# Pooled attention and routed experts: VectorE's value sums as one strided reduction instead of a chain of additions

## Chip, cores and metric

The kernel runs on one core of a Trainium2 chip. The metric is the device time of one execution in microseconds; the time before is 616.48 us, the median of three runs (615.58 to 618.09). "PE" is TensorE's matmul, "PEld" its weight load, "DVE" VectorE, "ACT" ScalarE, "POOL" GpSimd and "SP" SyncE, as in the rows below.

## What is computed

Eight batches of attention (8 heads, 576 queries, head size 64) over keys and values that are first averaged in groups of 8, so that 72 are left, and then a layer of eight experts of which each token takes one:

```python
k_p = k.reshape(B, H, Sp, 8, D).mean(axis=3)
v_p = v.reshape(B, H, Sp, 8, D).mean(axis=3)
attn = softmax(q @ k_p.T / sqrt(D));  x = attn @ v_p      # 4608 tokens x 512
e_idx = argmax(x @ w_gate)
out = gate_w * sigmoid(x @ w_output_gate)[e_idx] * (relu(x @ w1[e_idx]) @ w2[e_idx])
```

The change touches only how the eight values of a group are summed (the division by 8 is done elsewhere).

## The kernel before

**Attention.** The 4608 queries are 36 tiles of 128. Each tile is worked in two halves (four heads each), so there are 72 half steps, and the code writes them out in the order in which every engine runs its part. In a half step PE computes the scores of tile i (line 266, into one of three banks p_h), transposes the probabilities of tile i-2 (line 286) and computes the value product of tile i-3 (line 294, into bank p_y[0] or p_y[1] by the half). VectorE takes the maximum of the scores (`peak`, line 272), and for tile i-3 the reciprocal of the row sums (`values`, line 310) and the product with it (`normalise`, line 316, output xg). ScalarE computes the exponentials and copies the transposed probabilities. A bank p_y is free for the value product two half steps later once line 316 has read it.

**Values.** The values of one batch lie in the buffer `vt` (a view of the tensor that the rows call `rows`): for each half `a` (0 or 1) and each of three groups `c` of partitions, 512 words, which are 8 neighbouring values of 64 words. Their sum is `vp` (3 x 64 words for each half). There is one buffer `vt`: SyncE's load of the next batch (`load_v`, line 191, six DMAs) waits until the last sum has read it, and behind it in SyncE's queue stand the loads of queries (line 187) and keys (line 183).

For batches 1 to 7 the first of three halvings is done by GpSimd (`halve_v`, line 225: three additions 128x256 for each half a). The other two are VectorE's (`pool_v`, line 229): four partial sums become two (`n = 2 * D`), and two become one (`n = D`, into `vp`). For batch 0 VectorE does all three (`first_v`), in the kernel's start.

**Order.** The generator `pooled` gives VectorE's additions of one batch one by one to a queue of spare work; `work(n)` takes n pieces from it, and a half step calls it with 2 pieces behind the maximum, 1 behind the value product and 1 behind the normalisation (`WORK = (2, 1, 1)`). `pooled(b)` is put at the head of the queue. Behind it stand the pieces of `route`, which choose the expert of a group of four tiles. The sum `vp` is then read by PE (`turn_v`, line 244) and ScalarE (`place_v`, line 239).

**After attention.** GpSimd has written the normalised rows into the experts' order (line 434), the last group's routing makes a table of jobs, and the expert stage (from 187 us on) runs over that table with PE's two layers (lines 1015 and 996).

Of the kernel before, what the change touches and what calls it, by code (L numbers as in the profile page):

```python
# [15 lines left out]
ALU = mybir.AluOpType  # L16
AX = mybir.AxisListType
PSUM = bass.MemoryType.PSUM

B, H, S, D = 8, 8, 576, 64  # L20
KEYS, POOL = 72, 8
# [75 lines left out]
def attention_and_routing(ctx, tc, sh, qT, kT, v, wg, wst, xs):  # L97
    nc = tc.nc
# [11 lines left out]
    vt = sh.rows[:, 0:6 * DM].rearrange("p (a c f) -> p a c f", a=2, c=3)  # L110
# [68 lines left out]
    k_t, vp_t, vT_t = {}, {}, {}  # L179
# [45 lines left out]
            nc.gpsimd.tensor_tensor(vt[:, a, c, 0:256], vt[:, a, c, 0:256], vt[:, a, c, 256:512], op=ALU.add)  # L225

    def pool_v(b, a, n):
        to = vt[:, a, :, 0:n] if n > D else vp_t[b][:, :, a]
        nc.vector.tensor_tensor(to, vt[:, a, :, 0:n], vt[:, a, :, n:2 * n], op=ALU.add)

    def first_v(a):
        if a == 0:
            vp_t[0] = p2.tile([P, 3, 2, D], F32, tag="vp", name="vp0", bufs=1)
        for n in (4 * D, 2 * D, D):
            pool_v(0, a, n)

    def place_v(b, c):
        for h in range(2):
# [282 lines left out]

    def pooled(b):
        for a in range(2):
            for n in (2 * D, D):
                pool_v(b, a, n)
                yield 0

    tick = [0]

# [14 lines left out]
    for b in range(1, B):  # L544
        f = S * b // P + 0.5 * (b % 2)
        at(f - 8.5, load_k, b)
        at(max(f - 5, 0), load_v, b)
        at(f - 4.5, load_q, b)
        for m in range(9):
            at(max(f - 5.5, 0) + 0.5 * (m // 2), add_k, b, *((4 >> m // 4, m % 4, m % 4 + 1) if m < 8 else (1, 0, 4)))  # L550
        at(max(f - 2.5, 1.5), scale_k, b)
        for a in range(2):
            at(f - 2.5 + 0.5 * a, halve_v, b, a)
        at(f - 2, lambda b: queue.insert(0, [pooled(b), 0, -1]), b)
        for c in range(3):
            at(f - 0.5 + 0.5 * c, place_v, b, c)
        at(f - 0.5, turn_v, b)
        at(f + 1.5, gate_v, b)
# [24 lines left out]
    prepare_counts()  # L583
    ready_k(0)
    first_v(0)
    at(-0.5, ready_k, 1)
    at(-0.5, first_v, 1)
    at(1.5, prepare_routing)
    for c in range(3):
# [822 lines left out]
```

## Time and profile before

| what | value |
|---|---|
| median of three runs | 616.48 us (615.58 to 618.09) |
| the profiled execution's own time | 617.31 us |
| its span, first to last instruction | 615.6 us |
| busy: PE, VectorE, ScalarE, GpSimd | 581.6, 361.5, 260.0, 234.6 us |
| attention with its start | to about 165 us |
| expert stage | from about 187 us |

The span leaves out 1.7 us around the first and the last instruction. A busy share is an average over stages with different limits, so the rows further down are taken from single stretches. Times in rows are in microseconds from the span's start, unless they are said to be ns. A bracket at a row's end is the time for which the engine sat idle before it, and what ended it. [...]

### The profile page before, as it was taken

How to read it: one execution, taken by the hardware profiler on the slowest of the kernel's cores; microseconds unless marked ns; L12 is line 12 of the kernel's file. 1: busy time of each engine (PE TensorE's matmuls, PEld its weight loads, DVE VectorE, ACT ScalarE, POOL GpSimd, SP SyncE). 2: the span in 40 equal slices, each digit the busy share in tenths (PEclk: the TensorE clock that was granted, in tenths of full speed). 3: DMA queues.
4: the chain of work that ended last, by engine and by line, in shares of the span. 5: the costliest groups of instructions: out<-in, count | busy, mean ns of one | idle time of the engine just before them, and what ended most of it. 6: DMA issues, size and time to landing. Idle time of an engine off the chain costs nothing.

```text
span 615.6 us, 12478 instructions
## 1 busy us (share of the span) xinstructions
PE 581.6 (94%) x3543; PEld 531.6 (86%) x3544; DVE 361.5 (59%) x836; ACT 260.0 (42%) x693; POOL 234.6 (38%) x348
## 2 busy tenths in 40 slices
PE   0899999998898999999989999999999999999996
PEld 0899998887897989899879988989898898989895
DVE  5678899877986823699377513376143843333232
ACT  2798887788542511367235201244031520211110
POOL 3667889782444533134131222212121331212031
PEclk9999999999999999999989999999999999999999
DMA  9878789899576641748848413073223203020112
GB/s 260 281 233 281 255 282 345 314 323 284 170 249 194 199 145 37 219 137 292 254 156 255 139 44 70 17 230 129 80 41 117 70 5 83 17 68 17 52 35 68
DMA packets 52622, 99.20 MB, mean 161 GB/s; under 512 B 7406, under 2 KB 31982, under 8 KB 50736
## 3 DMA queue, kind: packets, MB, share of 16 engines
q1 hardware_dynamic: 44560, 76.62, 41.5%
q0 software_dynamic: 7968, 21.63, 9.6%
q14 instruction: 72, 0.59, 0.3%
q8 instruction: 22, 0.36, 0.3%
HBM read 74.03 MB, written 25.51 MB: 162 GB/s over the span
## 4 chain that ended last, share of the span: by engine, by line
PE 64%; issue 3%; DVEq 1%; DVE 1%; POOL 0%; ACT 0%; POOLq 0%
PE p_h L1015 33%; PE p_y L996 30%; PE p_y L649 1%; DVEq L1189 0%; DVE rows L1186 0%; POOL out L1329 0%; DVE xt L1159 0%; DVEq L754 0%; DVE p_y L83 0%; DVEq L1158 0%; ACT xt L1086 0%; DVEq L774 0%; DVE ht L1195 0%; PE p_y L1052 0%; DVE sums L1213 0%
## 5 line engine op out<-in xcount | busy, mean ns | idle before, releaser
L1102 ACT ACTIVATE ht<-p_h 128x384 fp32r<-128x384 f32 (+1 forms) x104 | 46.8, 450 | 237.0 <-PE p_h L1015 226.4
L1329 POOL DMA_INDIRECT out<-rows,dst x41 | 42.2, 1030 | 209.5 <-DVE rows L1186 207.2
L1015 PE MATMUL p_h<-xt,w1b 128*128 128x384 f32 (+1 forms) x736 | 117.2, 320 | 3.3 <-DVE ht L1195 2.7
L1015 PEld LDWEIGHTS p_h<-xt,w1b 128*128 128x128 f32 x736 | 116.0, 192 | 4.5 <-DVE ht L1195 2.9
L996 PE MATMUL p_y<-w2b,ht 128*128 128x512 f32 x480 | 110.4, 390 | 0.0
L996 PEld LDWEIGHTS p_y<-w2b,ht 128*128 128x128 f32 x480 | 89.8, 188 | 18.4
L1195 DVE SCALAR_TENSOR_TENSOR ht<-p_h,ht 128x384 fp32r<-128x384 f32 (+1 forms) x104 | 52.3, 503 | 89.0 <-ACT ht L1102 82.2
L996 PE MATMUL p_y<-w2a,ht 128*128 128x512 f32 x408 | 94.5, 390 | 0.7 <-PE p_y L649 0.4
L1015 PE MATMUL p_h<-xt,w1a 128*128 128x256 f32 (+1 forms) x640 | 93.6, 306 | 0.6 <-DVE sums L1213 0.6
L1015 PEld LDWEIGHTS p_h<-xt,w1a 128*128 128x128 f32 x640 | 92.9, 190 | 1.4 <-DVE sums L1213 0.8
L1186 DVE TENSOR_SCALAR rows<-p_y,sc 128x512 f32<-128x512 f32 x41 | 30.6, 750 | 104.6 <-PE p_y L996 87.5
L996 PEld LDWEIGHTS p_y<-w2a,ht 128*128 128x128 f32 x408 | 76.1, 188 | 17.1 <-issue 1.6
L277 ACT ACTIVATE p<-p_h,m 128x72 f32<-128x72 f32 x288 | 71.4, 367 | 21.2 <-DVE m L272 20.8
L294 PE MATMUL p_y<-vbd,pT 128*128 128x162 f32 (+1 forms) x480 | 73.5, 306 | 6.1 <-DVE xg L316 4.4
L294 PEld LDWEIGHTS p_y<-vbd,pT 128*128 128x128 f32 (+1 forms) x480 | 60.7, 179 | 9.8 <-issue 5.9
L1306 POOL DMA_INDIRECT xm<-xs,src x54 | 55.8, 1034 | 26.4 <-POOL src L1302 13.4
L434 POOL DMA_INDIRECT xs<-xg,where x36 | 37.0, 1029 | 30.1 <-PE p_y L294 8.5
L210 POOL TENSOR_TENSOR kq<-kq 128x288 f32<-128x288 f32 (+1 forms) x63 | 41.3, 682 | 15.5 <-DMA kq<-kT 14.1
L266 PE MATMUL p_h<-kbd,q_even 128*128 128x144 f32 (+1 forms) x160 | 29.7, 314 | 14.5 <-DMA q_even<-qT 11.7
L287 ACT ACTIVATE pT<-ptr 128x384 f32<-128x384 f32 x72 | 38.0, 530 | 2.6 <-PE ptr L286 1.6
L266 PEld LDWEIGHTS p_h<-kbd,q_even 128*128 128x128 f32 (+1 forms) x160 | 23.8, 199 | 15.9 <-issue 12.1
L286 PE MATMUL ptr<-ident,p 128*128 128x128 f32 x216 | 36.4, 278 | 0.1
(174 smaller groups left out, 667.4 us busy)
## 6 DMA issues: line engine op xcount, KB each, us to landing
stage<-wst SPq DMA_DIRECT2D x64, 512.0 KB
kq<-kT SPq DMA_DIRECT2D x7, 1152.0 KB
rows<-xs SPq DMA_DIRECT2D x40, 192.0 KB
rows<-v SPq DMA_DIRECT2D x16, 288.0 KB
kq<-qT SPq DMA_DIRECT2D x4, 1152.0 KB
rows<-xs SPq DMA_DIRECT2D x64, 64.0 KB
q_even<-qT SPq DMA_DIRECT2D x3, 1152.0 KB
xs<-stage SPq DMA_DIRECT2D x8, 321.0 KB
```

The source lines that it names most:

```text
L210: nc.gpsimd.tensor_tensor(k[:, :, 0:w], k[:, :, 0:w], k[:, :, w:2 * w], op=ALU.add)
L266: nc.tensor.matmul(s[r0:r0 + n, 144 * c:144 * c + 144], q_t[b][:, 2 * a + c, s0:s0 + n], kbd[b % 2][:, 2 * a + c, :], start=True, stop=True)
L277: nc.scalar.activation(pt[i % 3][:, 4 * a + h, 0:KEYS], sv[:, h], AF.Exp, bias=m[:, h:h + 1])
L287: nc.scalar.activation(pT_t[i][:, 3 * a:3 * a + 3, :], tr[:, 0:384].rearrange("p (c n) -> p c n", c=3), AF.Copy)
L294: nc.tensor.matmul(av[r0:r0 + n, COLS * c:COLS * c + 2 * COLS], pT[:, 3 * a + c, r0:r0 + n], vbd[b % 2][:, a, c].rearrange("p h f -> p (h ...
L434: ins = nc.gpsimd.indirect_dma_start(out=xs, out_offset=bass.IndirectOffsetOnAxis(ap=where, axis=0), in_=x.bitcast(I32), in_offset=None)
L996: i = mm(to, ht[:, h, f, P * k:P * k + P], w[:, part, o:o + DM], start=(f == 0 and part == 0 and h == 0), stop=(f == 7 and h == 1))
L1015: i = mm(to, w[:, part, o:o + P], x, start=(d == 0 and k == 0), stop=(d == 3 and k == len(terms) - 1))
L1102: act(ht[:, 0, f, 0:n], p_h[f % 3][:, 0:n], AF.Relu).then_inc(q["hh"], 1)
L1195: nc.vector.scalar_tensor_tensor(ht[:, 1, f, 0:n], src, 0.0, ht[:, 0, f, 0:n].bitcast(F32), op0=ALU.max, op1=ALU.subtract).then_inc(q["hl" ...
L1306: nc.gpsimd.indirect_dma_start(out=xb[:, k].bitcast(I32), out_offset=None, in_=pairs_of, in_offset=bass.IndirectOffsetOnAxis(ap=src[:, k:k ...
L1329: nc.gpsimd.indirect_dma_start(out=out, out_offset=bass.IndirectOffsetOnAxis(ap=dst[:, k:k + 1], axis=0), in_=yb[2 if k == size - 1 else k ...
```

## The change

`pool_v` sums all partial sums of a half in one instruction, a `tensor_reduce` over a view in which the partial sums are the innermost axis (step 64 words) and the 64 words of a value the next one. Batch 0 sums 8 values per result in one instruction for each half where three additions stood; batches 1 to 7 sum 4 where two additions stood. GpSimd's halving stays as it is. `pooled` gives two pieces of work instead of four.

```diff
     def pool_v(b, a, n):
-        to = vt[:, a, :, 0:n] if n > D else vp_t[b][:, :, a]
-        nc.vector.tensor_tensor(to, vt[:, a, :, 0:n], vt[:, a, :, n:2 * n], op=ALU.add)
+        nc.vector.tensor_reduce(vp_t[b][:, :, a], vt[:, a, :, 0:n].rearrange("p c (r d) -> p c d r", d=D), axis=AX.X, op=ALU.add)

     def first_v(a):
...
-        for n in (4 * D, 2 * D, D):
-            pool_v(0, a, n)
+        pool_v(0, a, POOL * D)
...
     def pooled(b):
         for a in range(2):
-            for n in (2 * D, D):
-                pool_v(b, a, n)
-                yield 0
+            pool_v(b, a, POOL // 2 * D)
+            yield 0
```

On VectorE in the kernel's start, around the two sums of batch 0 (kq are keys, m the maxima of scores, the numbers after a name tell tiles apart), the order of before and then of after:

```order
L229 TENSOR_TENSOR rows<-rows 128x3x256
L229 TENSOR_TENSOR rows<-rows 128x3x128
L229 TENSOR_TENSOR vp_151<-rows 128x3x64
L272 TENSOR_REDUCE m_0_157<-p_h 128x4
L206 TENSOR_TENSOR kq<-kq 128x2x288
L206 TENSOR_TENSOR kq<-kq 128x2x144
L206 TENSOR_TENSOR kq<-kq 128x2x72
L229 TENSOR_TENSOR rows<-rows 128x3x256
L229 TENSOR_TENSOR rows<-rows 128x3x128
L229 TENSOR_TENSOR vp_151<-rows 128x3x64
L272 TENSOR_REDUCE m_1_174<-p_h 128x4
```

Here only the additions go and nothing else changes its place; the same stretch of VectorE after:

```order
L228 TENSOR_REDUCE vp_151<-rows 128x3x64
L270 TENSOR_REDUCE m_0_155<-p_h 128x4
L206 TENSOR_TENSOR kq<-kq 128x2x288
L206 TENSOR_TENSOR kq<-kq 128x2x144
L206 TENSOR_TENSOR kq<-kq 128x2x72
L228 TENSOR_REDUCE vp_151<-rows 128x3x64
L270 TENSOR_REDUCE m_1_170<-p_h 128x4
```

Each maximum m still follows directly on a sum. On VectorE in batch 6's sums, as in every batch from 1 to 7 (grec is the reciprocal, xg the normalisation), before:

```order
L229 TENSOR_TENSOR rows<-rows 128x3x128
L229 TENSOR_TENSOR vp_1623<-rows 128x3x64
L310 RECIPROCAL grec_1482<-p_y 128x4
L229 TENSOR_TENSOR rows<-rows 128x3x128
L316 TENSOR_TENSOR xg_1480<-p_y,grec_1482 128x320
L229 TENSOR_TENSOR vp_1623<-rows 128x3x64
L272 TENSOR_REDUCE m_1_1685<-p_h 128x4
```

The reciprocal and the normalisation stood between the additions of the first half and the last addition of the second; VectorE at the same place after:

```order
L228 TENSOR_REDUCE vp_1609<-rows 128x3x64 x2
L308 RECIPROCAL grec_1468<-p_y 128x4
L314 TENSOR_TENSOR xg_1466<-p_y,grec_1468 128x320
L270 TENSOR_REDUCE m_1_1669<-p_h 128x4
```

Now both halves' sums stand ahead of them, next to each other. Two line numbers less are the lines that the change takes out.

## Rows read from the trace of the kernel before

**Rows 1.** The page: the span, and the clock granted to TensorE in 40 slices of it (tenths of full speed, 9 is 90% or more).

```profile
span 615.6 us, 12478 instructions
PEclk9999999999999999999989999999999999999999
```

**Rows 2.** Busy time of each engine (with the number of instructions) in three stretches, in us from the span's start: attention, the passage to the experts, the experts. The last columns are the granted clock, the share of the DMA engines' time and GB/s.

```profile
18.00:140.00 122.00, 116.58 (x944) 108.59 (x942) 103.74 (x335) 100.38 (x381) 97.47 (x139) 1.00 0.87 290
140.00:187.00 47.00, 42.41 (x291) 39.27 (x291) 37.96 (x152) 28.82 (x86) 17.98 (x19) 1.00 0.67 219
187.00:615.60 428.60, 419.09 (x2299) 380.57 (x2299) 208.90 (x322) 126.72 (x216) 113.81 (x162) 1.00 0.38 114
```

**Rows 3.** Who waited for whom between 12 and 187 us: us in total, times, the longest in us.

```profile
DVE rows L229 <- POOL rows L225: 5.1, 6, 2.5
PE p_y L294 <- DVE xg L316: 4.4, 5, 1.5
```

**Rows 4.** The same view for the DMA queue of SyncE, up to 190 us.

```profile
SPq L191 <- DVE vp L229: 80.3, 7, 13.7
```

**Rows 5.** Groups of VectorE instructions up to 200 us with their shapes apart: output and input size, count, busy us, mean ns of one, idle us before them. The 128x768 additions are batch 0's first ones.

```profile
L332 DVE TENSOR_REDUCE lg<-xg 128x64 f32<-128x512 f32 x9 | 6.1, 676 | 0.0
...
L229 DVE TENSOR_TENSOR rows<-rows 128x768 f32<-128x768 f32 x2 | 1.9, 954 | 4.3 <-DMA rows<-v 4.3
L671 DVE TENSOR_REDUCE rows<-rows 128x100 f32<-128x700 f32 x1 | 1.5, 1509 | 0.0
L671 DVE TENSOR_REDUCE rows<-rows 128x12 f32<-128x84 f32 x1 | 0.3, 313 | 0.0
```

**Rows 6.** The timeline of all engines in the start: start us, duration us, engine, line, operation, count of merged instructions.

```profile
11.01 1.55 DVE L229 TENSOR_TENSOR rows<-rows 128x768 f32<-128x768 f32 x2 [4.28 <-DMA rows<-v]
...
12.60 0.36 DVE L229 TENSOR_TENSOR vp<-rows 128x192 f32<-128x192 f32 x1
...
13.46 1.58 DVE L206 TENSOR_TENSOR kq<-kq 128x576 f32<-128x576 f32 x3
...
14.96 1.54 DVE L229 TENSOR_TENSOR rows<-rows 128x768 f32<-128x768 f32 x2
...
15.78 2.29 PE L266 MATMUL p_h<-kbd,q_even 128*128 128x144 f32 x8 [2.74 <-ACT kbd L215]
16.54 0.36 DVE L229 TENSOR_TENSOR vp<-rows 128x192 f32<-128x192 f32 x1
16.92 1.15 SPq L191 DMA_DIRECT2D rows<-v  x3
17.15 0.46 DVE L272 TENSOR_REDUCE m<-p_h 128x4 f32<-128x288 f32 x1 [0.26 <-PE p_h L266]
```

**Rows 7.** Groups of VectorE's additions between 20 and 140 us, which are those of batches 1 to 7 (columns as in rows 5).

```profile
L229 DVE TENSOR_TENSOR vp<-rows 128x192 f32<-128x192 f32 x14 | 11.0, 785 | 0.2
L229 DVE TENSOR_TENSOR rows<-rows 128x384 f32<-128x384 f32 x14 | 9.5, 678 | 5.1 <-POOL rows L225 5.1
```

**Rows 8.** The timeline in batch 2's sums (VectorE, and PE's value product).

```profile
44.51 0.55 DVE L229 TENSOR_TENSOR rows<-rows 128x384 f32<-128x384 f32 x1
45.09 0.36 DVE L229 TENSOR_TENSOR vp<-rows 128x192 f32<-128x192 f32 x1
45.37 0.17 DVE L310 RECIPROCAL grec<-p_y 128x4 f32<-128x4 f32 x1
45.46 1.12 DVE L229 TENSOR_TENSOR rows<-rows 128x384 f32<-128x384 f32 x1
...
46.50 0.48 DVE L316 TENSOR_TENSOR xg<-p_y,grec 128x320 f32<-128x320 f32 x1
46.90 0.55 DVE L229 TENSOR_TENSOR vp<-rows 128x192 f32<-128x192 f32 x1
...
47.69 0.99 PE L294 MATMUL p_y<-vbd,pT 128*128 128x162 f32 x6
```

**Rows 9.** The timeline in batch 5's sums.

```profile
95.38 0.55 DVE L229 TENSOR_TENSOR rows<-rows 128x384 f32<-128x384 f32 x1
...
95.96 2.68 DVE L229 TENSOR_TENSOR vp<-rows 128x192 f32<-128x192 f32 x1
...
96.32 2.09 POOL L225 TENSOR_TENSOR rows<-rows 128x256 f32<-128x256 f32 x3
...
98.66 0.52 DVE L229 TENSOR_TENSOR rows<-rows 128x384 f32<-128x384 f32 x1
99.10 0.48 DVE L316 TENSOR_TENSOR xg<-p_y,grec 128x320 f32<-128x320 f32 x1
...
99.73 1.06 PE L294 MATMUL p_y<-vbd,pT 128*128 128x162 f32 x6 [0.90 <-DVE xg L316]
```

**Rows 10.** The timeline in batch 7's sums.

```profile
133.16 0.56 DVE L229 TENSOR_TENSOR rows<-rows 128x384 f32<-128x384 f32 x1 [0.42 <-POOL rows L225]
...
136.73 0.56 DVE L229 TENSOR_TENSOR rows<-rows 128x384 f32<-128x384 f32 x1 [2.52 <-POOL rows L225]
...
137.20 0.48 DVE L316 TENSOR_TENSOR xg<-p_y,grec 128x320 f32<-128x320 f32 x1
...
137.83 1.07 PE L294 MATMUL p_y<-vbd,pT 128*128 128x162 f32 x6 [1.49 <-DVE xg L316]
```

**Rows 11.** All instructions of line 332: count, then the shortest, median and longest in ns.

```profile
L332 DVE TENSOR_REDUCE lg<-xg x9: 665/676/686, 40.5 to 166.3; 128x64 f32<-128x512 f32 x9
```

## Prediction

> **What bounds the kernel now.** I read the page first: TensorE is at its full clock throughout, so what moves the time is when TensorE works, not how fast it is clocked [rows 1]. The windows by stage say where it works: in the attention stage (18 to 140 us) PE is busy for 116.58 of 122 us while VectorE is busy for 103.74 and GpSimd for 97.47, so three engines are close to full at once; in the expert stage PE is busy for 419.09 of 428.60 us [rows 2]. The expert stage does not touch the changed code and starts when attention has routed its last tokens. So a delay of attention is paid in full at the end, and what counts is whether PE in attention is delayed.
>
> Who waits for VectorE there? The list of waits shows PE's value product waiting for the normalisation of VectorE (xg, line 316), 4.4 us in five waits, and VectorE itself waiting 5.1 us for GpSimd's halving of the values (line 225) [rows 3]. SyncE's queue waits for the pooled values too: the load of the next batch's values, and behind it in the same queue those of its queries and of the keys after it, is held until the last pooling sum has read the buffer, 80.3 us in seven waits [rows 4].
>
> **The cost of one new instruction.** The change replaces two-input additions by a sum over a strided innermost axis: four (or eight) elements, 64 words apart, per result. The trace has no such sum of this size. Two rows bound it. The sum of line 332 reads runs of four adjacent words: 676 ns for 512 elements. The sum of line 671 reads seven elements 56 words apart: 313 ns for 84 elements and 1509 ns for 700 [rows 5]. From the latter, (1509 - 313) / (700 - 84) = 1.94 ns an element and 150 ns fixed; line 332 less the same 150 ns gives 1.03 ns an element. The new sum steps 64 words for every element and has no adjacent run, so it is nearest to line 671 and I take 1.94 ns; both ends stay in the range. Then the sum over four (768 elements) takes 150 + 768 x 1.94 = 1.64 us, at the fast end 0.95 us; the sum over eight (1536) takes 3.13 us, at the fast end 1.74 us.
>
> [...]
>
> **First batch.** The order shows three additions per half replaced by one sum, twice, with nothing else moved between them. Before, the first half runs from 11.01 to 12.96 us, 1.95 us end to end, and the second from 14.96 to 16.90 [rows 6]. Each becomes 3.13 us, so each grows by 1.18 us. Both are on the path: behind the first stand, on VectorE, the maximum of the first scores and the key additions at 13.46 that release the second half of the scaled keys and so PE's scores at 15.78; behind the second stand the next maximum at 17.15, which then had waited only 0.26 us for PE, and the load of batch 1's values on SyncE at 16.92. So the first delays PE by 1.2 us and the second VectorE and the loads by another 1.2, less that 0.26 us. That would be 2.1 us for VectorE and 2.4 us for the loads; I take +2.2 us, with -0.4 us (2 x (1.74 - 1.95)) at the fast end.
>
> **Batches 1 to 7.** In busy time little happens: before, 14 additions of each size took 9.5 + 11.0 = 20.5 us [rows 7], after, 14 sums of 1.64 us take 23.0. What happens in one place matters more. Before, the four additions of a batch were interleaved with the reciprocal and the normalisation of a tile; after, each batch's two sums stand next to each other, ahead of both. The second sum also waits for GpSimd to halve the second half, and the reciprocal now waits behind that.
>
> Batch 2 is the mild case: GpSimd was done, the additions began at 44.51, the reciprocal came at 45.37, the normalisation was over at 46.98, and PE wrote the next product into that bank at 47.69, not delayed [rows 8]. After, two sums end at 44.51 + 3.28 = 47.79; reciprocal and normalisation need 0.17 + 0.48 us, 0.7 with their gap, so the bank is free at 48.5 and PE starts about 0.85 us late.
>
> Batch 5 is the usual late case: the second addition was stretched to 2.68 us while GpSimd halved the second half until 98.41, the normalisation ended at 99.58 and PE, already waiting, started at 99.73 [rows 9]. After, the first sum ends at 97.02, the second starts at 98.41 and ends at 100.05, the normalisation at 100.75: +1.2 us. Batch 6 has the same pattern and I give it the same. In batch 7 VectorE waited for GpSimd until 136.73 and PE started at 137.83 [rows 10]; after, the second sum ends at 138.37, the normalisation at 139.07, against 137.68: +1.4 us.
>
> Batches 1 to 4 lie between batch 2 and batch 5 (in 3 and 4 PE was waiting for VectorE a little already); I take 0.9 us each. Sum: 4 x 0.9 + 2 x 1.2 + 1.4 = 7.4 us. VectorE gets its extra load back in the steps after a batch, but PE, which works without a gap there, cannot catch up. The loads of a later batch move with the sums that release them, and have room: SyncE waited 80.3 / 7 = 11.5 us for each release [rows 4]. The routing steps that share the queue of spare VectorE work come two slots earlier, and one rank product on PE half a tile earlier; both are the same instructions, their inputs are ready, and I cost that at nothing. If an input were late there, PE would wait for one small VectorE step, such as the reciprocal's 0.17 us.
>
> **The sum.** 2.2 + 7.4 = +9.6 us on the profiled execution's 617.31 us (615.6 us of it are the span). The median of the three runs shown, 616.48, is 0.83 us lower, so the forecast is 616.48 + 9.6 = 626.1, rounded to 626.0.
>
> **Rivals.**
> *Hidden after the first batch*: the sums are slow, but PE finds other work while VectorE is busy. For it: batch 2 had 0.7 us of slack. Against: in batches 5 and 7 PE was already waiting for the normalisation. It gives 616.48 + 2.2 = 618.7 and decides if the bank of the value product is not what PE needs next.
> *Full rate*: the strided sum runs at 1.03 ns an element. Against it stands line 671. Then the first batch gains 0.4 us, batch 2 loses nothing (44.51 + 1.9 + 0.7 = 47.1, before 47.69), batches 5 and 6 end at 98.41 + 0.95 + 0.7 = 100.06, +0.5 us each, batch 7 +0.7: +1.3 us, 617.8, because the second sum still waits for GpSimd ahead of the reciprocal.
> *The other side, faster*: before, the two-input additions were stretched by GpSimd, 20.5 us against 14 x (0.55 + 0.36) = 12.7 without it, while no sum of line 332 ever took longer than 0.69 us [rows 7, 8, 11]. If the sums run at full rate and nothing waits for GpSimd any more, PE's 4.4 us of waits for the normalisation go, and 0.4 us at the start: 616.48 - 4.8 = 611.7. It decides from the point where a sum costs less than the two additions with their stretch, 20.5 / 14 = 1.46 us; 1.64 is above it. [...]
> That the change does not do what it says is excluded by the order: 34 additions go, 16 sums come.
>
> **How the numbers follow.** Forecast 0.70 (622 to 629), hidden 0.11, full rate 0.13, faster 0.06. The upper end: no slack anywhere, 2.4 + 7 x 1.4 = 12.2, 628.7, rounded to 629.5. The lower end takes in the full-rate case, 617.8, rounded to 617.5. That leaves out the faster case and about 0.1 of tails. A measurement of this kernel can tell about 0.5%, 3.1 us, from no change: 613.4 to 619.6 is "same". The forecast's whole range is slower, and so is a third of the hidden case, where a batch or two cost something after all; the rest of it and the full-rate case are the same. Slower 0.74, same 0.20, faster 0.06.
>
> **What would show it.** In the profile after: sums over four near 1.64 us and over eight near 3.1 us; the load of batch 1's values on SyncE about 2.3 us later than 16.92; PE waiting for the normalisation once per batch, in total some 10 us instead of 4.4; the attention stage longer by 9 to 10 us and the expert stage as long as before. Sums near 0.95 us would prove me wrong at the first step; sums of 1.64 us with PE's waits unchanged at the second.

## The result, and the profile after

The changed kernel takes 621.83 us (median of six runs, 620.76 to 624.01), the kernel before, run beside it, 616.79 (615.58 to 618.86). The ratio is 1.0069, 95% interval 1.0048 to 1.0091: +4.3 us (3.0 to 5.6). The forecast was 626.0, slower by 9.5; the direction was right, the size about double. The profiled execution of after is the longest of its six (624.01, span 622.2), so its rows show where time goes better than how much.

First the price. Groups of VectorE instructions up to 200 us in the changed kernel, columns as in [rows 5]:

```profile
L228 DVE TENSOR_REDUCE vp<-rows 128x192 f32<-128x768 f32 x14 | 20.8, 1495 | 6.8 <-POOL rows L225 6.7
...
L228 DVE TENSOR_REDUCE vp<-rows 128x192 f32<-128x1536 f32 x2 | 5.5, 2752 | 5.3 <-DMA rows<-v 5.3
```

A sum over four takes 1.50 us where 1.64 was forecast, over eight 2.75 where 3.13 was: (2752 - 1495) / 768 = 1.64 ns an element, not 1.94. In batches 1 to 7 the busy time is as good as unchanged, 20.8 us after against 11.0 + 9.5 before [rows 7].

Busy time by stage, the same stretches as [rows 2]:

```profile
18.00:140.00 122.00, 112.60 (x902) 105.21 (x902) 101.23 (x312) 97.91 (x370) 90.41 (x133) 0.99 0.80 269
140.00:187.00 47.00, 41.83 (x308) 38.49 (x307) 38.51 (x155) 28.93 (x94) 22.14 (x25) 1.00 0.74 242
187.00:622.20 435.20, 425.69 (x2332) 386.30 (x2330) 213.99 (x331) 129.78 (x221) 111.94 (x163) 1.00 0.39 116
```

From 18 to 140 us PE is busy 4.0 us less than before (116.58) and gets 42 instructions less done; VectorE and GpSimd are less busy too. No engine is busier there than before; the stretch holds less work, and the waits below say where the time goes. Who waits, between 20 and 187 us (us in total, times, longest), beside [rows 3]:

```profile
PE p_y L292 <- DVE xg L314: 6.8, 7, 2.0
DVE vp L228 <- POOL rows L225: 6.7, 8, 1.8
...
PE p_y L292 <- DVE grec L308: 1.4, 1, 1.4
```

PE's wait for the normalisation, and once for the reciprocal ahead of it, rises from 4.4 to 8.2 us.

The chain of waits shows how far the passage to the experts moved: the same 33 matmuls of PE, before and then after.

```profile
186.92 7.74 PE p_y L649 x33
```

```profile
194.51 7.76 PE p_y L646 x33
```

That is +7.59 us, of which 6.6 are left at the end of the span. PE's transposes of a batch's pooled values (tile vtr, one group per batch) give a mark in each batch; their start in the two traces:

| batch | before | after | later by | grown by |
|---|---|---|---|---|
| 0 | 17.87 | 19.44 | 1.57 | 1.57 |
| 1 | 31.80 | 35.40 | 3.60 | 2.03 |
| 2 | 48.52 | 52.69 | 4.17 | 0.57 |
| 3 | 65.31 | 70.31 | 5.00 | 0.83 |
| 4 | 82.57 | 88.46 | 5.89 | 0.89 |
| 5 | 100.63 | 107.59 | 6.96 | 1.07 |
| 6 | 119.77 | 127.84 | 8.07 | 1.11 |
| 7 | 138.74 | 146.72 | 7.98 | -0.09 |

The last column is what PE lost or won back between two marks, and not only what the sums of that batch cost. Batch 5's 1.07 shows it. PE was 5.89 us late at the product of batch 4 and 6.95 at that of batch 5, but 0.88 of this came half way, at a rank product of the routing (tile rk). VectorE's routing step ahead of it (tile zs), before and then after, and PE's wait after:

```profile
88.99 0.65 DVE L350 TENSOR_TENSOR zs<-lg,oh 128x32 f32<-128x32 f32 x1
```

```profile
94.97 1.62 DVE L348 TENSOR_TENSOR zs<-lg,oh 128x32 f32<-128x32 f32 x1
...
97.75 0.18 PE L354 MATMUL rk<-oh,tri 128*128 128x40 bf16 x1 [0.72 <-ACT pT L285]
```

Both times GpSimd was adding keys beside zs. The step took 1.62 us in the four profiles in which a batch takes two turns of the queue and routing comes earlier (after, experiments 2, 4 and 5), and PE was 0.87 to 0.91 us later behind it in each; it took 0.65, and PE lost nothing there, in experiments 1, 3, 6, 7 and 9, which keep four turns. In those four, GpSimd goes on with key additions where before a scatter (line 434) stood between them, so the earlier routing also moved work in GpSimd's queue. That this is what stretched zs is not shown.

**The start.** The timeline of after (values landed 1.0 us later in this execution than in that of before; landings lie between 11.0 and 12.0 us over the profiles, experiment 8 aside):

```profile
12.01 2.75 DVE L228 TENSOR_REDUCE vp<-rows 128x192 f32<-128x1536 f32 x1 [5.28 <-DMA rows<-v]
...
16.54 2.76 DVE L228 TENSOR_REDUCE vp<-rows 128x192 f32<-128x1536 f32 x1
...
17.36 2.29 PE L264 MATMUL p_h<-kbd,q_even 128*128 128x144 f32 x8 [3.42 <-ACT kbd L215]
...
19.32 1.15 SPq L191 DMA_DIRECT2D rows<-v  x3
...
30.06 0.31 PE L264 MATMUL p_h<-kbd,kq 128*64 128x144 f32 x1 [1.91 <-ACT p L275]
```

The load of batch 1's values is issued at 19.32 us, 2.4 later than in [rows 6], 1.0 of it the late landing. Behind it in SyncE's queue stand batch 1's queries, and PE's first scores of batch 1 at 30.06 need them (2.03 us later than before; the trace names ACT there, in another run of this start the DMA of the queries).

**Batch 5**, after, against [rows 9]:

```profile
101.91 1.52 DVE L228 TENSOR_REDUCE vp<-rows 128x192 f32<-128x768 f32 x1
102.32 2.09 POOL L225 TENSOR_TENSOR rows<-rows 128x256 f32<-128x256 f32 x3
...
104.44 1.48 DVE L228 TENSOR_REDUCE vp<-rows 128x192 f32<-128x768 f32 x1 [1.01 <-POOL rows L225]
...
106.05 0.49 DVE L314 TENSOR_TENSOR xg<-p_y,grec 128x320 f32<-128x320 f32 x1
...
106.68 1.06 PE L292 MATMUL p_y<-vbd,pT 128*128 128x162 f32 x6 [1.38 <-DVE grec L308]
```

From the end of GpSimd's halving to PE's product there were 99.73 - 98.41 = 1.32 us; now there are 106.68 - 104.41 = 2.27. A whole sum of 1.48 us stands ahead of the normalisation where one addition of 0.52 us stood. This is the forecast's mechanism, line by line.

**Batch 7**, after, against [rows 10]:

```profile
143.60 1.45 DVE L228 TENSOR_REDUCE vp<-rows 128x192 f32<-128x768 f32 x1 [1.76 <-POOL rows L225]
...
145.18 0.49 DVE L314 TENSOR_TENSOR xg<-p_y,grec 128x320 f32<-128x320 f32 x1
145.81 1.06 PE L292 MATMUL p_y<-vbd,pT 128*128 128x162 f32 x6 [2.01 <-DVE xg L314]
```

Here the same thing happens: from the start of the second half's work to PE's product it takes 2.21 us instead of 1.10, but GpSimd was ready at 143.60, only 6.87 us later than before. PE's product just ahead of this one, before and then after:

```profile
134.23 0.99 PE L294 MATMUL p_y<-vbd,pT 128*128 128x162 f32 x6
```

```profile
141.69 0.99 PE L292 MATMUL p_y<-vbd,pT 128*128 128x162 f32 x6
```

PE was 8.06 us late at the product of batch 6, 7.46 here and 7.98 at the product of batch 7. It had won back 0.6 us in the steps between, and batch 7 cost 0.52 of it again.

### The profile page after: what moved, and what is told of

It is laid out like the page before. It is cut to its first block, busy times and chain, and to the rows that moved or that the text cites. A ratio compares the mean times of both kernels' runs of the same rounds, so it can differ in the third digit from the quotient of the medians.

```text
span 622.2 us, 12453 instructions
## 1 busy us (share of the span) xinstructions
PE 582.1 (94%) x3543; PEld 531.6 (85%) x3544; DVE 364.5 (59%) x818; ACT 260.3 (42%) x693; POOL 229.9 (37%) x348
## 4 chain that ended last, share of the span: by engine, by line
PE 64%; issue 3%; DVEq 1%; DVE 1%; ACT 0%; POOL 0%; ACTq 0%; POOLq 0%
PE p_h L1012 33%; PE p_y L993 30%; PE p_y L646 1%; DVEq L1186 0%; ACT xt L1083 0%; DVE rows L1183 0%; POOL out L1326 0%; DVE xt L1156 0%; DVEq L751 0%; DVE p_y L83 0%; DVEq L771 0%; PE p_y L1049 0%; DVE ht L1192 0%; DVE sums L1210 0%; ACTq L1082 0%
## 5 line engine op out<-in xcount | busy, mean ns | idle before, releaser
L292 PE MATMUL p_y<-vbd,pT 128*128 128x162 f32 (+1 forms) x480 | 74.0, 307 | 10.1 <-DVE xg L314 6.8
L1303 POOL DMA_INDIRECT xm<-xs,src x54 | 54.0, 999 | 26.4 <-POOL src L1299 13.4
```

The lines of the kernel that those rows point to most:

```text
L292: nc.tensor.matmul(av[r0:r0 + n, COLS * c:COLS * c + 2 * COLS], pT[:, 3 * a + c, r0:r0 + n], vbd[b % 2][:, a, c].rearrange("p h f -> p (h ...
L1303: nc.gpsimd.indirect_dma_start(out=xb[:, k].bitcast(I32), out_offset=None, in_=pairs_of, in_offset=bass.IndirectOffsetOnAxis(ap=src[:, k:k ...
```

## Experiments

All ratios are to the kernel before, run beside each on the same chip; a ratio of 1.001 is 0.62 us.

**1. The first batch alone**, and **2. the other batches alone.** The changed first_v on the kernel before (its sum is called sum_v there); then the changed pooled on the kernel before.

```diff
-        for n in (4 * D, 2 * D, D):
-            pool_v(0, a, n)
+        sum_v(0, a, POOL * D)
```

> Only batch 0 is summed by the strided sum over eight, batches 1 to 7 keep their additions in their old places. Theory 1 (each part pays for its own): the two sums are 0.8 us longer each (2.75 against 1.95 us), both on the path: 1.6 us slower, ratio 1.0026. Rival 2 (all of the loss comes from the start): 5 us slower, ratio 1.008. Rival 3 (the loss is the order of batches 1 to 7): no change, 0 to 0.5 us.

```diff
-            for n in (2 * D, D):
-                pool_v(b, a, n)
-                yield 0
+            sum_v(b, a, POOL // 2 * D)
+            yield 0
```

> Only batches 1 to 7 are summed by the strided sum over four, two sums next to each other; batch 0 keeps its additions. Theory 1: 3.4 us slower, ratio 1.0055 (the changed kernel's 5.0 less 1.6). Rival 2: no change. Rival 3: 5 us slower, ratio 1.008.

Measured: first batch alone 1.0030 (1.0010 to 1.0050), +1.9 us; the other batches alone 1.0063 (1.0040 to 1.0085), +3.9 us. Each part pays for its own; that all of the loss comes from the start, or none of it, falls. Together they would be 5.8, the change has 4.3 (3.0 to 5.6); the intervals allow that they add up.

**3. The sums in the additions' old places.** As 2, with a second empty turn of the queue behind each sum, so that the second half's sum stands behind the reciprocal and routing keeps its turns. **4. The additions in the sums' places.** The kernel before, with one turn for both additions of a half: all four stand ahead of the reciprocal, and routing comes two turns earlier.

```diff
-            for n in (2 * D, D):
-                pool_v(b, a, n)
-                yield 0
+            sum_v(b, a, POOL // 2 * D)
+            yield 0
+            yield 0
```

> As the kernel with only batches 1 to 7 changed, but each batch's second sum stands behind the reciprocal, where the additions of the second half stood, and the spare-work queue gives as many turns as before. Theory 1 (sums of 1.5 us and their order both count): between 1 and 2.5 us slower than before, since the reciprocal is freed of the second sum but the normalisation is not. Rival 3 (order alone): no change or up to 2 us faster, since GpSimd can no longer stretch VectorE's additions. If the length of the sums alone counts: as slow as the lumped one, about 3.4 us.

```diff
             for n in (2 * D, D):
                 pool_v(b, a, n)
-                yield 0
+            yield 0
```

> All additions stay, but those of batches 1 to 7 are put in the changed kernel's order: four additions next to each other ahead of the reciprocal, two turns of the queue instead of four. Theory 1: about 1 to 2 us slower. Rival 2: no change. Rival 3 (order alone): 4 to 5 us slower, as the changed kernel.

Measured: 1.0043 (1.0026 to 1.0061), +2.7 us, and 1.0054 (1.0035 to 1.0074), +3.3 us. Both are above what the theory gave (the first by little). 2.7 + 3.3 is more than the 3.9 of both together, though with their intervals only just. So the price and the place do not look like two terms that add: either one is enough to put something longer ahead of the normalisation.

**9. Which half of the fourth experiment's edit it was.** The four additions next to each other, but four turns kept, so that routing and its rank products on PE stay where they were.

```diff
             for n in (2 * D, D):
                 pool_v(b, a, n)
-                yield 0
+            yield 0
+        for _ in range(2):
+            yield 0
```

> All additions kept, in batches 1 to 7 all four of a batch next to each other ahead of the reciprocal, as the changed kernel's sums stand, but four turns of the queue kept, so that routing and its rank products on PE stand where they stood before (in the fourth experiment, +3.3 us, they came two turns earlier). If the lump ahead of the reciprocal makes the loss: +3 us again, ratio 1.005. If the routing two turns earlier made it: 0, ratio 1.000. If both do: +1 to +2 us, ratio 1.002 to 1.003.

Measured: 1.0070 (1.0042 to 1.0098), +4.3 us. The lump makes a loss without the earlier turns. In the time those turns show no cost: +3.3 with them, +4.3 without, the intervals overlap, and the granted clock of the six executions here was 0.993 on average against 0.996 in experiment 4. In the traces they show one: the 0.9 us at the rank product is there in experiment 4 and not here. Its waits, in the view of [rows 3] between 20 and 187 us:

```profile
PE p_y L294 <- DVE xg L316: 8.0, 7, 2.1
DVE rows L229 <- POOL rows L225: 5.6, 6, 2.6
```

PE waits 8.0 us for the normalisation, as in the changed kernel, without a single strided sum.

**7. Is a delay of the start passed on?** As 1, with each of the first batch's two sums run twice.

```diff
-        sum_v(0, a, POOL * D)
+        for _ in range(2):
+            sum_v(0, a, POOL * D)
```

> Only the first batch changed, as in the first experiment (that alone cost +1.85 us), and each of its two sums over eight run twice, so 2 x 2.75 = 5.5 us more of VectorE's time at the start; the rest as before. Theory 1 (a delay of the start is passed on in full): +1.85 + 5.5 = +7.3 us, ratio 1.012. Rival (a part of every delay is given back later, as the 6.6 of 7.6 us in the profiles): about two thirds to 0.85 of it, +5 to +6 us, ratio 1.008 to 1.010. Rival (the first batch's loss was the fallen clock alone, not the delay): +3 us or less, ratio 1.005.

Measured: 1.0120 (1.0091 to 1.0148), +7.4 us against 1.9 + 5.5 = 7.4. The time fits a delay that is passed on in full, but the interval (5.6 to 9.1 us) just touches the rival's 5 to 6. The trace says more: PE is 7.55 us late at the mark of batch 1, 7.41 at that of batch 7 and 6.67 at the start of the experts, so a delay from the start is kept through attention, and 0.7 us is given back in the passage.

**5. Adjacent words.** The changed kernel in every respect, but the values are stored so that the four numbers of a sum are neighbours (a transposition of the input array's layout; GpSimd's halving is the same).

```diff
-        "v": c(v).reshape(B, H, KEYS, POOL * D),
+        "v": c(v.reshape(B, H, KEYS, 2, 4, D).transpose(0, 1, 2, 3, 5, 4)).reshape(B, H, KEYS, POOL * D),
...
-        nc.vector.tensor_reduce(vp_t[b][:, :, a], vt[:, a, :, 0:n].rearrange("p c (r d) -> p c d r", d=D), axis=AX.X, op=ALU.add)
+        to = vp_t[b][:, :, a]
+        if n == 4 * D:
+            nc.vector.tensor_reduce(to, vt[:, a, :, 0:n].rearrange("p c (d r) -> p c d r", r=4), axis=AX.X, op=ALU.add)
+        else:
+            nc.vector.tensor_reduce(to, vt[:, a, :, 0:n].rearrange("p c (s d r) -> p c d s r", s=2, r=4), axis=AX.XY, op=ALU.add)
```

> The changed kernel whole (one sum per half, same order, same queue turns), but the values are laid out in memory so that the four numbers of a sum are adjacent words instead of 64 words apart; the first batch's sum over eight reads two adjacent runs of four. Only the price of a sum changes. If the step of 64 words is what the sums pay for, a sum over four goes from 1.50 us to about 0.95 us (line 332's 1.03 ns an element) and over eight from 2.75 to about 1.7. Theory 1 (each part pays for its own): the start's loss goes to about 0 or -0.4, of the 3.9 us of batches 1 to 7 some 14 x 0.55 = 7.7 us of VectorE's time is taken off and the loss falls to about +0.5 to +1.5: ratio 1.000 to 1.003. Rival (the order of batches 1 to 7 alone makes their loss): the additions in that order still cost +3.3, so this kernel stays at +3: ratio 1.005. Rival (the step does not matter): sums stay near 1.5 us, ratio 1.007.

Measured: 0.9979 (0.9964 to 0.9994), -1.3 us. The groups of its sums:

```profile
L230 DVE TENSOR_REDUCE vp<-rows 128x192 f32<-128x768 f32 x14 | 13.2, 948 | 10.1 <-POOL rows L225 10.1
...
L232 DVE TENSOR_REDUCE vp<-rows 128x192 f32<-128x1536 f32 x2 | 3.5, 1748 | 4.7 <-DMA rows<-v 4.7
```

0.95 and 1.75 us, the fast end of the prediction's bound (0.95 and 1.74). The step through memory is more than all of the loss: with the same order and 1.04 ns an element instead of 1.67 the change is a small gain. VectorE now stands 10.1 us waiting for GpSimd. Nor is it the price alone that tells these sums from experiment 4's additions, which stand in the same place and turns: two additions of 0.55 and 0.36 us cost as much as one sum of 0.95, yet that kernel lost 3.3 us (the first batch is worth 0.4 of the difference). Those additions were stretched beside GpSimd, up to 2.45 us for one in experiment 4, while the fourteen sums here took 0.94 to 0.95 each.

**6. Adjacent words in the old places** (as 5, with the second empty turn of experiment 3), and **10. the same, half a tile later.** At the later place GpSimd has mostly halved the values when VectorE comes to them.

> As the kernel with adjacent words, but in batches 1 to 7 the second half's sum stands behind the reciprocal, where an addition stood before, and the routing keeps its old turns. A sum of some 0.95 us takes the place of two additions of 0.66 and 0.72 us (with GpSimd's stretch). Theory 1: VectorE saves 14 x 0.4 = 6 us, the normalisation waits less, PE's 4.4 us of waits for it fall; faster than before by 1 to 3 us, ratio 0.995 to 0.998. Rival (PE is held by GpSimd's halving, not by VectorE's sums): ratio 0.999 to 1.001.

```diff
-        at(f - 2, lambda b: queue.insert(0, [pooled(b), 0, -1]), b)
+        at(f - 1.5, lambda b: queue.insert(0, [pooled(b), 0, -1]), b)
```

> The kernel with adjacent words and the second sum behind the reciprocal, but both sums of batches 1 to 7 half a tile later in the program, when GpSimd has halved the values. In that kernel VectorE stood 9.7 us waiting for GpSimd in front of the normalisation. Theory (what hurts is whatever makes VectorE late for the normalisation, the wait for GpSimd included): the wait for GpSimd falls to about 3 us, PE's 4.4 us for the normalisation to about 2, another 1.5 to 3 us faster: ratio 0.990 to 0.993. Rival (PE then waits for the pooled values or for the transposes of them instead): ratio 0.995 to 0.998.

Measured: 0.9952 (0.9936 to 0.9969), -3.0 us, and 0.9910 (0.9889 to 0.9931), -5.5 us, 611.47 us against 616.98: the fastest kernel of this study. The waits of experiment 10, between 20 and 187 us:

```profile
DVE vp L230 <- POOL rows L225: 1.0, 2, 0.7
...
PE vtr L246 <- DVE vp L230: 0.8, 1, 0.8
...
PE p_y L296 <- DVE xg L318: 0.4, 1, 0.4
```

PE's 4.4 us for the normalisation are down to 0.4, and VectorE's wait for GpSimd is 1.0; PE comes to the experts 4.86 us earlier than in the kernel before. In experiment 6 PE still waits 4.4 us for the normalisation and comes to the experts only 0.94 us earlier; the rest of its gain lies in the expert stage, 425.7 us there against 428.7 before, which the change does not touch. One fall of the clock, worth about 1.7 us, is in the latter and none in the former (last section); what made up the remainder is open.

**11. The strided sums half a tile later** (the changed kernel with the second empty turn and the edit of 10), and **12. the additions half a tile later** (the kernel before with the edit of 10 alone).

> The changed kernel with its strided sums, first batch too, but in batches 1 to 7 the second sum stands behind the reciprocal and both half a tile later. Theory (lateness for the normalisation): the start's +1.8 us stays, the batches' +3.9 shrink to +0.5 to +1.5, ratio 1.003 to 1.005. Rival (the longer sums cost VectorE's time wherever they stand): ratio 1.007 to 1.008.

> The kernel before with nothing changed but the place: the additions of batches 1 to 7 half a tile later, when GpSimd has halved the values. It tells how much of the 5.5 us gained by adjacent words, half a tile later, comes from the place alone. Theory (lateness for the normalisation): VectorE's 5.1 us of waiting for GpSimd fall to about 1, the additions are no longer stretched by the halving, and PE's 4.4 us for the normalisation fall to about 1.5: 2 to 4 us faster, ratio 0.994 to 0.997. Rival (the gain came from the cheaper sums): ratio 0.999 to 1.001.

Measured: 1.0012 (0.9993 to 1.0032), +0.7 us, and 1.0010 (0.9989 to 1.0031), +0.6 us. The first is at the lower end of its theory's range or below it, and less than the first batch's 1.9 alone, so by the times the other batches lose little or nothing any more; its trace does not show that they gain, since PE still comes to the experts 3.91 us late and the expert stage is the shortest of all. The second refutes its theory, which had 2 to 4 us of gain. The waits of 12 say why:

```profile
PE vtr L244 <- DVE vp L229: 5.7, 5, 1.6
...
PE p_y L294 <- DVE xg L316: 0.8, 1, 0.8
DVE rows L229 <- POOL rows L225: 0.5, 1, 0.5
```

The wait for the normalisation went as expected (0.8), but PE now waits 5.7 us for the pooled values themselves: the last addition of a batch stands behind the normalisation and is over only when PE wants to transpose its result. In experiment 11 this wait is 5.1. Only the short sums of experiment 10 fit between the two, with 0.8. The place alone gains nothing, the price alone 3.0 us (experiment 6), both together 5.5.

**8. What a step costs.** The kernel before with 18 extra sums on VectorE at its start, 13 strided and 5 of adjacent words, on the zeroed buffer of the values (`x`).

```diff
...
+        def strided(n, step, run, m):
+            v = x[:, 0:n * m * step].rearrange("p (g r d) -> p g d r", g=n, r=m)[:, :, 0:run, :]
+            nc.vector.tensor_reduce(o[:, 0:n * run].rearrange("p (g d) -> p g d", g=n), v, axis=AX.X, op=ALU.add)
+
+        for n, step, run, m in ((3, 64, 64, 4), (3, 64, 32, 4), (3, 64, 32, 8), (12, 16, 16, 4), (6, 32, 32, 4), (3, 56, 56, 4),
+                                (1, 56, 50, 7), (1, 64, 50, 7), (2, 128, 96, 4), (1, 192, 192, 4), (12, 15, 15, 4), (3, 63, 63, 4), (3, 65, 64, 4)):
+            strided(n, step, run, m)
+        for n, m in ((192, 4), (96, 8), (96, 4), (110, 7), (192, 2)):
+            nc.vector.tensor_reduce(o[:, 0:n], x[:, 0:n * m].rearrange("p (d r) -> p d r", r=m), axis=AX.X, op=ALU.add)
...
```

> The kernel before with 18 extra strided sums on VectorE at its start, on the zeroed buffer of the values, to price one sum by itself (the time of the whole kernel is of no interest and some 20 us longer). Varied: the step between the words that are added (15, 16, 32, 56, 63, 64, 65, 128, 192 words and 1), how many are added per result (4, 7, 8) and how many results. Account A (every hop of more than one word has one price per element read): all strided sums of 768 elements take 1.5 us, whether over 4 or over 8, and 350 elements 0.75 us. Account B (the price is by the result as well as by the element): 768 elements over 8 (96 results) are 0.1 us faster than over 4 (192 results), and the sum over seven lies on one line with line 671. Account C (the step itself decides): 56 words cost 1.94 ns an element and 64 words 1.64, and other steps differ again. Adjacent words: 1.04 ns an element in every account.

The groups (L143 strided, L149 adjacent; the 192 results of the first line stand for steps of 16, 32, 64, 65, 128 and 192 words):

```profile
L143 DVE TENSOR_REDUCE vpb<-rows 128x192 f32<-128x768 f32 x6 | 8.7, 1448 | 0.2
...
L143 DVE TENSOR_REDUCE vpb<-rows 128x96 f32<-128x768 f32 x1 | 1.4, 1443 | 0.0
...
L143 DVE TENSOR_REDUCE vpb<-rows 128x168 f32<-128x672 f32 x1 | 1.3, 1292 | 0.0
...
L149 DVE TENSOR_REDUCE vpb<-rows 128x192 f32<-128x768 f32 x1 | 1.0, 953 | 0.0
...
L143 DVE TENSOR_REDUCE vpb<-rows 128x96 f32<-128x384 f32 x1 | 0.8, 801 | 0.0
...
L149 DVE TENSOR_REDUCE vpb<-rows 128x96 f32<-128x384 f32 x1 | 0.6, 553 | 0.0
```

And the two sums over seven, 56 and then 64 words apart, in the timeline:

```profile
12.98 0.80 DVE L143 TENSOR_REDUCE vpb<-rows 128x50 f32<-128x350 f32 x1
```

```profile
13.81 0.74 DVE L143 TENSOR_REDUCE vpb<-rows 128x50 f32<-128x350 f32 x1
```

Strided: (1443 - 801) / 384 = 1.67 ns an element and 159 ns fixed, over four or over eight, at any of the steps; adjacent: (953 - 553) / 384 = 1.04 and 153. That is account A, with one exception: seven words 56 apart cost (800 - 159) / 350 = 1.83, while four words 56 apart cost (1292 - 159) / 672 = 1.69 and seven words 64 apart (740 - 159) / 350 = 1.66. Line 671, the row behind the forecast, sums seven words 56 apart: it pays for something particular to that pattern. What that is stays open, and the 1.94 of line 671 itself was not reached.

## Why the prediction was half right

**The price of a sum: 1.94 ns an element was the wrong row.** "It is nearest to line 671" judged by the step; in experiment 8 the step made no difference (1.66 to 1.69 ns an element from 15 to 192 words), and line 671's pattern is the dear exception (1.83 for seven words 56 apart). Measured 1.50 and 2.75 us against 1.64 and 3.13. With the measured price the prediction's own sum is about 7.6 us instead of 9.6: 1.5 for the first batch (between 2 x 0.80 and the same less the 0.26 of PE), 0.7 for each of batches 1 to 4, 1.03 each for 5 and 6 (98.41 + 1.50 + 0.70 - 99.58), 1.25 for batch 7.

**First batch, +2.2: right in kind, and in size with some luck.** Its price was too high; by the measured one the term is 1.5. Alone it measured +1.9 (0.6 to 3.1), which covers both. A part of it that the prediction lacked is the granted clock, which fell to 0.50 behind PE's longer pause in the profiles of after and of experiment 1 (last section).

**A delay of attention is paid in full: right within the interval.** Experiment 7. That only 6.6 of 7.59 us were left in the profiled run belongs to the expert stage, whose length from those 33 matmuls to the end lies between 425.4 and 428.7 us over the fourteen profiles, with no relation to the delay: 428.7 in the kernel before and in experiment 12 (2.39 us late), 428.2 in experiment 7 (6.67 us late), 427.7 in after, 425.4 in experiment 11 (3.91 us late).

**Batches 1 to 7, +7.4: right in kind, 3.9 (2.5 to 5.2) in size.** PE waits for the normalisation behind the sums in each batch. Where nothing else comes between, the cost is near what the measured price gives: 0.57 in batch 2 (0.52 by the price of 1.50), 0.93 at the product of batch 6 (1.03), and 0.74 in batch 1 (0.7). Batch 1 cannot be read in after, where the start's delay runs into it; in the profile of experiment 2 PE begins batch 1's scores 0.09 us later than in before (28.12 against 28.03) and reaches its mark 0.83 later (32.63 against 31.80).

What failed beside the price is the adding up, the terms **"2 x 1.2 + 1.4"** and the sentence that PE **"cannot catch up"**. Each term was read from the times of before, as if GpSimd and PE were late by the same amount. In batches 5 and 7 GpSimd had slipped less than PE, so a part of the wait was already paid by the delay from before: from the product of batch 4 to that of batch 5 the sums added 0.2 us beside the 0.88 of the routing step, and batch 7 added 0.5, where the measured price gives 1.03 and 1.25. And PE did catch up: 0.6 us between batches 6 and 7 (in experiment 2 as well, 5.31 to 4.71), and 0.39 from the mark of batch 7 to the start of the experts in after. Why it could is open. These two make up some 2.5 us, against which stands the routing step's 0.9; with the price's 2.0 that brings 9.6 to about 6, near the 5.8 of experiments 1 and 2 added, and above the 4.3 (3.0 to 5.6) of the change. The rest is not explained.

**The rivals.** Hidden after the first batch: it falls, since the other batches alone cost 3.9 us (experiment 2) and PE waits for the normalisation in them. Full rate: experiment 5 is that very case, sums of 0.95 us in the changed order; it gained 1.3 us where the rival had a loss of 1.3. Faster: its decision point, a sum cheaper than 1.46 us, fits 1.50 on one side of it (+4.3) and 0.95 on the other (-1.3), though two points do not place it, and at the later place sums of 1.50 lose next to nothing (experiment 11). Its 4.8 us came only with the place changed as well (-5.5): in experiment 5 PE still waits for the normalisation behind sums that wait for GpSimd. As that rival had it, the sums did not take GpSimd's stretch here: the fourteen of after take between 1.45 and 1.55 us, one of them (1.52) beside GpSimd's halving in batch 5, where an addition of before took up to 2.68 [rows 9].

**Edits costed at nothing.** The routing's two turns: not borne out by the traces, which show 0.9 us at the rank product wherever routing comes earlier, and not refuted by the times (experiments 4 and 9). The price that the prediction gave for an input that is late, 0.17 us, was too low for it. The loads of later batches: no wait of PE for them shows behind batch 1.

## What to carry to other kernels

An operation that replaces two shorter ones must be priced by its own access pattern: take the row that reads memory in the same way, not the one that is nearest in step, and give the rows' spread to the range (line 332 gave 1.03 ns an element here, line 671 1.94, and the sum took 1.64). In a queue that feeds another engine, what counts is how much stands ahead of the instruction that the other engine waits for, waits included, and not the busy time: 20.5 and 20.8 us of work on VectorE differed by 3.9 us. Moving work past that instruction helps only as far as its own consumer allows. Losses read one by one from a trace of before are not simply to be added: once the consumer is late, a producer that is less late has paid a part of the next one.

## What the hardware showed that was not expected

The pause of PE ahead of batch 1's scores had a price beyond its own length. Stretches of after (PE busy and instructions, PEld, VectorE, ScalarE, GpSimd, granted clock, DMA share, GB/s):

```profile
30.00:31.00 1.00, 0.94 (x9) 0.77 (x10) 0.61 (x1) 0.48 (x3) 0.36 (x1) 1.00 1.03 433
31.00:32.00 1.00, 1.00 (x7) 1.00 (x6) 0.96 (x3) 0.49 (x1) 0.00 (x0) 0.69 0.65 256
32.00:33.00 1.00, 1.00 (x7) 0.66 (x7) 0.96 (x4) 0.11 (x1) 0.17 (x1) 0.50 0.18 33
33.00:34.00 1.00, 1.00 (x8) 0.61 (x7) 0.60 (x2) 0.84 (x4) 1.00 (x2) 0.50 0.64 180
34.00:35.00 1.00, 1.00 (x7) 1.00 (x6) 0.32 (x1) 0.41 (x2) 1.00 (x2) 0.60 0.59 166
35.00:36.00 1.00, 1.00 (x11) 1.00 (x10) 0.37 (x2) 1.00 (x6) 1.00 (x3) 1.00 0.77 236
```

After an idle time of 1.91 us the granted clock fell to 0.50 between 31 and 35 us, which cost, as an estimate from these rows, 0.31 + 0.50 + 0.50 + 0.40 = 1.7 us in that execution. The same came after 2.0 us in experiment 1, 2.2 in experiment 11 and 1.8 in experiment 3; not after 1.92 in experiment 7, 1.74 in experiment 6, 1.07 in experiment 2 and 1.2 in the kernel before.

It is not peculiar to the start. The profile of before has such a fall in the expert stage, the 8 in [rows 1], where the prediction took the clock as full throughout. It stands behind an idle time of 2.68 us:

```profile
310.60 1.75 PE L1015 MATMUL p_h<-xt,w1b 128*128 128x256 f32 x10 [2.68 <-DVE ht L1195]
```

```profile
312.00:313.00 1.00, 1.00 (x6) 1.00 (x6) 1.00 (x2) 0.18 (x1) 0.00 (x0) 0.50 1.03 209
```

Eight of the fourteen profiles have one near this place, and their expert stages take 427.3 to 428.7 us; the other six take 425.4 to 427.8. In the profiles of before and after each fall, up to the last microseconds, stands just behind an idle time of PE: 2.68 us in before, 1.91 in after and 1.73 ahead of a second one at 318 us. But not every such idle time brought one (1.92 us in experiment 7 did not); why is open. The times go with it: in experiment 1 the four executions with a mean granted clock of 0.999 or more took 616.5 to 618.2 us, the six at 0.994 or less 619.5 to 622.9. So a part of a small difference between kernels can be the clock's. As an estimate, 0.001 of the mean clock is 0.6 us of these 617; it was 0.996 in the executions of after, 0.999 in those of experiment 10 and 0.997 in those of before beside it.

In experiment 8 a strided sum cost 1.66 to 1.69 ns an element at every step tried from 15 to 192 words, 1.6 times the 1.04 of neighbours; only seven words 56 apart cost more (1.83). A transposition of the input's layout was therefore worth 5.6 us here (+4.3 to -1.3).
